# Thirty-four matmuls of a zeroed tile in TensorE's queue around the first scores

## The chip, the cores and the metric

The kernel runs on one core of one Trainium2 chip, in one launch. The metric is the device time of an execution in microseconds (us); the kernel before was timed three times.

## The reference

The layer takes x (8 batches, 8 heads, 512 tokens of 64) and a state of 32 rows for each batch and head, and computes in three steps:

```
scores  = x @ state.T / 8        a  = softmax(scores)     xread = a  @ state
scores2 = state @ x.T / 8        a2 = softmax(scores2)    sread = a2 @ x
x1 = concat(xread, sread) over tokens: (8, 544, 512), heads side by side
h  = relu(pad(x1) @ w_in);  conv = 3-tap convolution of h over tokens
x2 = (h * sigmoid(conv)) @ w_out
xk, xr = mixes of x2 with itself one token earlier (mu_k, mu_r)
out = sigmoid(xr @ w_r) * (relu(xk @ w_k)**2 @ w_v)
```

There are 512 + 32 = 544 tokens in a batch. Everything is float32.

## The kernel before, in words

Every large product is made of three matmuls (`mm3`, lines 108 to 114): each operand is split into a high and a low part, and high x high (L112), high x low (L113) and low x high (L114) are added up in PSUM. So each weight block has to be split before it is used (`Weights.split`, L158 to L170: two passes on ScalarE, the others on VectorE), and each intermediate too.

Phase 1 goes over nine tiles of tokens t (one for each batch, and one for all sread rows) and eight blocks f of the hidden size: a slot (t, f). The attention of a batch is folded into the first product: `m` (tile p_m) is state x w_in, and hps = m.T @ a gives the hidden block without ever forming xread. A slot is `g1_main` (hps), `g1_a` (ReLU, L430, and the taps, L441 and L443), `g1_b` (the gate), `g1_c` (the split) and `g1_sec` (the product with w_out into the four acc tiles). Phase 2 does the same for the last step, with kps, ks, acc and rps.

The attention of a batch (class `Attention`): `scores` (L284) multiplies the state's columns with x_t, four heads into each of two tiles p_s, g = 0 and 1. x_t of a batch comes in four transfers (L200), two heads in each. The code takes heads 0, 4, 1, 5 and so on, which is chunk 0, 2, 0, 2, 1, 3, 1, 3. Each score is two matmul instructions, 16 in all. VectorE then transposes p_s in blocks (L305), takes maxima (L296, L308), subtracts, sums, and turns the result back (L340, L343) into `aring`, which hps reads.

PSUM has eight banks: four acc tiles, two of hps or kps, and a ring of two under the tag "at" (`Attention.at`), for p_m, transposes and sread, and for scores of later batches; the first scores borrow two acc tiles. `m_odd` is the SBUF tile of the blocks m of odd batches, first written for batch 1.

What sets the order: the code is a list of instructions with priorities. The Tile framework plans it with a simulation that has its own costs and sends, on each engine, the instruction that is due first among those that are ready. In the prologue (L614 to L644) the due times count up in the order of the code; in the main loop they are written: slot number x 1000 plus the stage's offset `STAGE` (0 for the main product, 5400 for `g1_sec` and `g2_sec`), or 500 x half-slot less a lead for attention and weights, all behind BASE. So the prologue is due before all else; where one of its instructions is not ready, a later one that is goes first. On the chip each engine then works off its queue in the order planned.

The prologue, in order: loads of state and x_t of batch 0, the first w_in block, conv, mu and the first w_out block (L614 to L619, all issued by SyncE); the identity (`make_identity`) and zeros for `aux` on GpSimd; then

```
    a = Attention(0, ap)
    a.scores([ps_acc.tile([P, 512], F32, tag=f"acc{g}", name="p_s") for g in range(G)])
    a.begin()
    win[0][1]()
    a.state()
    a.m(0, 0, 1)
```

that is the scores, a small memset, the split of w_in, the split of the state (into `aux`), and the first block of m; then the softmax of both tiles, the split of conv and the split of w_out.

Of the kernel before, what the change touches and what calls it, by code (L numbers as in the profile page):

```python
# [8 lines left out]
F32 = mybir.dt.float32  # L9
# [15 lines left out]

ATTEND = 3
M_PARTS = (-8, -4, 3, 8)


@with_exitstack  # L30
def tile_kernel(
# [26 lines left out]
    nc = tc.nc  # L58
    B, P, NST, H, D = x_n.shape
# [10 lines left out]
    N = 512  # L70
# [31 lines left out]
    m_odd = xp.tile([P, KF // 2, 2, G, 2 * P], F32R, tag="x16", name="m_odd")  # L102
# [497 lines left out]
    def at_half(k, *fns, prio=None):  # L600
        p = 500 * k - AHEAD if prio is None else prio
        half.setdefault(k, []).extend((fn, p) for fn in fns)
# [14 lines left out]
    vec.load()  # L617
    nc.sync.dma_start(out=muc, in_=mu)
    wout[0][0]()  # L619
    make_identity(nc, ident)  # L620
    nc.gpsimd.memset(aux[:, 1].bitcast(F32), 0.0)
    a = Attention(0, ap)
    a.scores([ps_acc.tile([P, 512], F32, tag=f"acc{g}", name="p_s") for g in range(G)])
    a.begin()
    win[0][1]()
    a.state()
    a.m(0, 0, 1)
# [18 lines left out]
    def attend(b, k, first):  # L646

        a_ = a if first else Attention(b, ap)
        if not first:
            at_half(k, a_.begin, a_.scores)  # L650
            if b == 1:
                at_half(M_PARTS[0] + 2 * KF - 1, a_.state)
            at_half(k + 1, lambda: a_.max1(0, nc.vector), lambda: a_.max1(1, nc.gpsimd))
# [6 lines left out]
            h = 2 * KF * b  # L660
            for q, d in enumerate(M_PARTS):
                if b == 1:
# [142 lines left out]
```

## Time and profile before

| | |
|---|---|
| three timed runs | 898.67, 899.1, 899.33 us, median 899.1 |
| profiled execution | 901.15 us, of which 899.2 are the span |
| TensorE, busy | 850.8 us of 4440 matmuls (95%) |
| VectorE / ScalarE / GpSimd, busy | 564.0 / 531.2 / 118.8 us |
| granted TensorE clock, mean | 0.974 of 2.4 GHz |

The profile is one execution. PE is TensorE's matmul side and PEld its weight loads, DVE is VectorE, ACT ScalarE, POOL GpSimd, SP SyncE. The span runs from the first to the last instruction; all times in rows are us from its start. A bracket at the end of a row gives how long the engine was idle before it, and what ended that. The chain of waits is followed back from the last instruction, at each step to what released it. Matmuls are pipelined: the distance between the starts of two is what one costs in a dense stream, and it is shorter than the duration of one.

### The profile page before, as it was taken

The numbers are of one execution on the slowest core, as the hardware profiler recorded it, in microseconds if no ns is written. First come the engines' busy times: TensorE is split into PE (matmuls) and PEld (weight loads), VectorE is DVE, ScalarE is ACT, GpSimd is POOL, SyncE is SP. The second block draws the span as 40 slices with busy tenths as digits, with TensorE's granted clock in tenths as the row PEclk, the third lists the DMA queues.
The fourth block names the chain that finished last, engine by engine and source line by source line (L and its number), as shares of the span: only waits on it lengthen the run. The fifth ranks groups of instructions, "written<-read, shape, count | busy, mean of one in ns | idle before, by whom it ended". The sixth has DMA issues, their size and how long they took to land.

```text
span 899.2 us, 12003 instructions
## 1 busy us (share of the span) xinstructions
PE 850.8 (95%) x4440; PEld 692.3 (77%) x4440; DVE 564.0 (63%) x950; ACT 531.2 (59%) x929; POOL 118.8 (13%) x223
## 2 busy tenths in 40 slices
PE   3749999999999997999999999999999999999997
PEld 1628777768777875789988888888888888888886
DVE  6899897699879987999784543523424244332221
ACT  4557686578577757777666755635556364553431
POOL 2313753342011112121000000000000000000000
PEclk7778999999999999999999999999999999999999
DMA  9682224544451537536731101111001111011010
GB/s 341 228 348 96 77 95 118 162 131 118 139 166 59 168 127 246 175 122 252 273 128 47 28 20 47 47 47 48 18 29 48 47 47 47 1 36 48 0 47 36
DMA packets 50842, 95.76 MB, mean 106 GB/s; under 512 B 9056, under 2 KB 31072, under 8 KB 48736
## 3 DMA queue, kind: packets, MB, share of 16 engines
q1 hardware_dynamic: 50784, 95.00, 32.0%
q8 instruction: 35, 0.57, 0.3%
q14 instruction: 23, 0.19, 0.1%
HBM read 64.54 MB, written 17.86 MB: 92 GB/s over the span
## 4 chain that ended last, share of the span: by engine, by line
PE 83%; DVE 8%; ACT 3%; issue 2%; DMA 2%; POOL 1%; SPq 0%; DVEq 0%; ACTq 0%; POOLq 0%
PE acc L113 13%; PE acc L114 13%; PE acc L112 13%; PE kps L112 7%; PE kps L113 7%; PE kps L114 7%; PE rps L114 3%; PE rps L113 3%; PE rps L112 3%; PE hps L112 3%; PE hps L114 3%; PE hps L113 3%; DVE cacc L443 2%; PE p_s L284 2%; PE p_m L113 1%
## 5 line engine op out<-in xcount | busy, mean ns | idle before, releaser
L568 DVE TENSOR_TENSOR ks<-k,ks 128x512 fp32r<-128x512 f32 (+1 forms) x72 | 47.7, 662 | 118.2 <-ACT ks L567 117.8
L443 DVE SCALAR_TENSOR_TENSOR cacc<-hb,vcol,cacc 128x512 f32<-128x512 f32 (+1 forms) x144 | 111.8, 788 | 15.5 <-ACT cacc L441 14.9
L113 PE MATMUL acc<-gs,out 128*128 128x512 f32 (+1 forms) x288 | 110.6, 386 | 0.0
L112 PE MATMUL kps<-xk,k 128*128 128x512 f32 (+1 forms) x288 | 110.0, 384 | 0.2 <-ACT k L554 0.2
L113 PE MATMUL kps<-xk,k 128*128 128x512 f32 (+1 forms) x288 | 110.2, 382 | 0.0
L114 PE MATMUL kps<-xk,k 128*128 128x512 f32 (+1 forms) x288 | 109.8, 382 | 0.0
L114 PE MATMUL acc<-gs,out 128*128 128x512 f32 (+1 forms) x288 | 109.6, 384 | 0.0
L112 PE MATMUL acc<-v,ks 128*128 128x512 f32 x272 | 106.0, 392 | 0.0
L113 PE MATMUL acc<-v,ks 128*128 128x512 f32 x272 | 105.9, 389 | 0.0
L114 PE MATMUL acc<-v,ks 128*128 128x512 f32 x272 | 105.7, 392 | 0.0
L112 PE MATMUL acc<-gs,out 128*128 128x512 f32 (+1 forms) x288 | 94.3, 389 | 4.3 <-ACT gs L459 4.3
L533 DVE SCALAR_TENSOR_TENSOR mix<-yt,muc,mix 128x384 f32<-128x384 f32 (+7 forms) x128 | 61.1, 500 | 47.7 <-ACT mix L531 47.2
L567 ACT ACTIVATE ks<-k 128x512 fp32r<-128x512 f32 (+1 forms) x72 | 43.6, 605 | 69.8 <-PE acc L114 69.6
L531 ACT ACTIVATE mix<-yt,om 128x384 f32<-128x384 f32 (+7 forms) x128 | 61.5, 517 | 32.2 <-DMA yt<-y 15.8
L554 ACT ACTIVATE k<-kps 128x512 f32<-128x512 f32 (+1 forms) x72 | 40.9, 569 | 48.9 <-PE kps L114 48.7
L112 PEld LDWEIGHTS acc<-gs,out 128*128 128x128 f32 x288 | 53.7, 192 | 16.1 <-ACT gs L459 6.1
L113 PEld LDWEIGHTS acc<-gs,out 128*128 128x128 f32 x288 | 54.8, 190 | 12.8 <-POOL hb L429 0.8
L114 PEld LDWEIGHTS acc<-gs,out 128*128 128x128 f32 x288 | 54.9, 191 | 10.8 <-issue 0.8
L112 PEld LDWEIGHTS kps<-xk,k 128*128 128x128 f32 x288 | 54.1, 188 | 10.8 <-ACT k L554 0.7
L113 PEld LDWEIGHTS kps<-xk,k 128*128 128x128 f32 x288 | 54.4, 189 | 10.1
L114 PEld LDWEIGHTS kps<-xk,k 128*128 128x128 f32 x288 | 54.3, 188 | 10.1
L451 ACT ACTIVATE g<-cacc 128x512 f32<-128x512 f32 (+1 forms) x72 | 43.8, 609 | 27.5 <-DVE cacc L443 19.4
(133 smaller groups left out, 1771.3 us busy)
## 6 DMA issues: line engine op xcount, KB each, us to landing
out<-r SPq DMA_DIRECT2D x34, 256.0 KB, 2.1
xT<-x_t SPq DMA_DIRECT2D x32, 256.0 KB, 4.0
xn<-x_n SPq DMA_DIRECT2D x8, 1024.0 KB, 5.4
y<-yo SPq DMA_DIRECT2D x8, 1024.0 KB, 4.8
me<-m SPq DMA_DIRECT2D x48, 128.0 KB, 2.4
m_odd<-m SPq DMA_DIRECT2D x48, 128.0 KB, 2.4
raw<-w_in SPq DMA_DIRECT2D x8, 512.0 KB, 6.0
raw<-w_out SPq DMA_DIRECT2D x8, 512.0 KB, 5.7
```

What stands on the lines that cost most here:

```text
L112: nc.tensor.matmul(ps, lh, rh, start=start and k == 0, stop=False)
L113: nc.tensor.matmul(ps, lh, rl, start=False, stop=False)
L114: nc.tensor.matmul(ps, ll, rh, start=False, stop=stop and k == last)
L284: nc.tensor.matmul(self.v["s", g][NS * j:NS * (j + 1), :], sT[self.b][r, h // 2, h % 2], xT[self.b][r, h // 2], start=True, stop=True,)
L443: nc.vector.scalar_tensor_tensor(a[:, :n], hb[:, k:k + n], w[k], a[:, :n], op0=ALU.mult, op1=ALU.add)
L451: nc.scalar.activation(g[:, :n], s["a"][:, :n], AF.Sigmoid)
L531: nc.scalar.activation(tmp[:, o:o + m], y[:, c, q - 1:q - 1 + m], AF.Copy, scale=om[:, i:i + 1])
L533: nc.vector.scalar_tensor_tensor(tmp[:, o:o + m], y[:, c, q:q + m], muc[:, i:i + 1], tmp[:, o:o + m], op0=ALU.mult, op1=ALU.add,)
L554: nc.scalar.activation(k[:, :n], s["p"][:, :n], AF.Relu)
L567: nc.scalar.activation(ks[:, 0, :n], s["k2"][:, :n], AF.Copy)
L568: nc.vector.tensor_tensor(ks[:, 1, :n], s["k2"][:, :n], ks[:, 0, :n].bitcast(F32), op=ALU.subtract)
```

## The change

A slice of `m_odd`, which nothing has written yet, is zeroed on GpSimd ahead of the identity. A function `idle(n)` takes a tile of the ring "at" and issues n matmuls of the zeroed slice with itself into it, 128x128 weights and 512 columns each, none of which is read. It is called with 4 ahead of the first scores and with 30 behind `a.begin()`. Nothing else is changed.

```diff
+IDLE_BEFORE, IDLE_AFTER = 4, 30
...
     wout[0][0]()
+    zeros = m_odd[:, 3].rearrange("p l g n -> p (l g n)")
+    nc.gpsimd.memset(zeros[:, :N].bitcast(F32), 0.0)
+
+    def idle(n):
+        p = a.at("p_z")
+        for i in range(n):
+            nc.tensor.matmul(p, zeros[:, :P], zeros[:, :N], start=True, stop=True)
+
     make_identity(nc, ident)
     nc.gpsimd.memset(aux[:, 1].bitcast(F32), 0.0)
     a = Attention(0, ap)
+    idle(IDLE_BEFORE)
     a.scores([ps_acc.tile([P, 512], F32, tag=f"acc{g}", name="p_s") for g in range(G)])
     a.begin()
+    idle(IDLE_AFTER)
     win[0][1]()
     a.state()
```

## Rows read from the trace of the kernel before

**Rows 1.** The page's first part: busy time, share of the span, instructions.

```profile
PE 850.8 (95%) x4440; PEld 692.3 (77%) x4440; DVE 564.0 (63%) x950; ACT 531.2 (59%) x929; POOL 118.8 (13%) x223
```

**Rows 2.** Chain of waits, 0 to 50 us: start, duration, what.

```profile
1.18 2.81 DMA xT<-x_t
...
4.12 5.53 PE p_s L284 x16
...
20.29 1.15 DVE in L170
...
21.48 0.48 PE p_m L113
...
26.44 0.53 PE hps L112
...
30.06 0.61 ACT hb L430
```

**Rows 3.** Timeline of VectorE: start, duration, instruction, idle time before it.

```profile
6.73 0.72 DVE L305 STREAM_TRANSPOSE q<-p_s 128x512 f32<-128x512 f32 x1 [6.73 <-PE p_s L284]
...
9.68 0.72 DVE L305 STREAM_TRANSPOSE q<-p_s 128x512 f32<-128x512 f32 x1 [1.07 <-PE p_s L284]
...
31.53 0.75 DVE L443 SCALAR_TENSOR_TENSOR cacc<-hb,vcol,cacc 128x512 f32<-128x512 f32 x1 [2.04 <-ACT cacc L441]
```

**Rows 4.** Stretches: us, busy time of five engines, granted clock, DMA.

```profile
12.00:13.00 1.00, 0.00 (x0) 0.00 (x0) 0.97 (x4) 1.00 (x2) 0.00 (x0) 1.00 1.05 398
...
14.00:15.00 1.00, 0.00 (x0) 0.00 (x0) 1.00 (x4) 1.00 (x5) 0.00 (x0) 0.50 0.99 397
```

**Rows 5.** Tile p_s, first scores and those near 50 us: ns min/median/max, starts.

```profile
L284 PE MATMUL p_s<-xT,sT x16: 1027/1057/1059, 4.1 to 8.6; 64*32 64x512 f32 x16
...
L284 PE MATMUL p_s<-xT,sT x16: 589/589/613, 49.3 to 50.6; 64*32 64x512 f32 x16
```

**Rows 6.** Timeline of TensorE's weight loads, 4 to 8.5 us.

```profile
4.76 0.18 PEld L284 LDWEIGHTS p_s<-xT,sT 64*32 64x32 f32 x4 [0.45 <-DMA xT<-x_t]
6.44 0.19 PEld L284 LDWEIGHTS p_s<-xT,sT 64*32 64x32 f32 x4 [1.50 <-DMA xT<-x_t]
7.71 0.18 PEld L284 LDWEIGHTS p_s<-xT,sT 64*32 64x32 f32 x4 [1.08 <-DMA xT<-x_t]
```

**Rows 7.** Timeline of TensorE's matmuls, 28 to 32 us.

```profile
28.48 0.63 PE L112 MATMUL hps<-aring,me 128*128 128x512 f32 x1
...
29.76 0.63 PE L112 MATMUL hps<-aring,me 128*128 128x512 f32 x1
...
31.18 0.39 PE L112 MATMUL hps<-aring,me 128*128 128x512 f32 x1
...
31.64 0.40 PE L114 MATMUL hps<-aring,me 128*128 128x512 f32 x1
```

**Rows 8.** Timeline of GpSimd, 0 to 3.2 us.

```profile
0.73 0.20 POOL masks.py:197 MEMSET ident<- 128x128 f32 x1 [0.29 <-POOLq L794]
0.87 1.81 POOL L621 MEMSET aux<- 128x2048 f32 x1
2.62 0.13 POOL L293 MEMSET s<- 128x1 f32 x2
2.78 0.29 POOL masks.py:199 TENSOR_SCALAR_AFFINE_SELECT ident<-ident 128x128 f32<-128x128 f32 x1
```

**Rows 9.** TensorE, 400 to 557.1 us: matmuls of tile kps, then of ks.

```profile
400.00:557.10 157.10, 63.55 (x276) 1.00 0.35 123
...
400.00:557.10 157.10, 46.82 (x192) 1.00 0.35 123
```

**Rows 10.** Timeline of TensorE's matmuls, 17 to 18 us.

```profile
17.63 0.69 PE L112 MATMUL p_m<-in,aux 128*128 128x128 f32 x2 [8.00 <-DVE in L165]
```

**Rows 11.** Timeline of VectorE, then of TensorE, 66 to 75.2 us.

```profile
66.77 0.42 DVE L275 TENSOR_TENSOR me<-p_m,me 128x256 fp32r<-128x256 f32 x1
...
74.92 0.39 PE L114 MATMUL hps<-aring,me 128*128 128x512 f32 x1
```

## The prediction, made before the change was run

> **What bounds the kernel now.** Read the busy table of the page first: TensorE has 95% of the span [rows 1], so nearly all the time is a dense matmul stream, and 34 more matmuls can shorten nothing in that stream itself. The change sits in front of that stream, so next comes the chain of waits over the first 50 us: a transfer of x_t until 3.99, the 16 score matmuls until 9.65, then VectorE (DVE) work, the first scaled weights at 20.29 to 21.44, the first m block on TensorE from 21.48, the first hps product from 26.44, and the first ReLU at 30.06 [rows 2]. In VectorE's timeline its idle time is in brackets: the second scores keep it waiting 1.07 us before 9.68; from there it is never idle until 29.49, and then waits 2.04 us for the ScalarE result behind the first hps product [rows 3]. So up to 29.49 the prologue is paced by VectorE, which starts when the scores end; a microsecond taken from the scores moves all of it.
>
> Why the scores end at 9.65 is seen in two views. The rows of the scores' weight loads give the landings of the four chunks of x_t: 4.12 for the first [rows 2], and loads that ended an idle time at 4.76, 6.44 and 7.71 [rows 6]. So 1.94 us pass between the last landing and the end. And one score matmul of that stretch lasts 1057 ns where the same tile at 49 to 51 us lasts 589 [rows 5]. The first ones therefore ran at the lower of the two levels, 1.2 GHz, although the page prints a granted clock of 1.00 for the start. The stretch at 12 to 13 us reads 1.00 with TensorE idle, that at 14 to 15 reads 0.50 [rows 4]: the clock reached 2.4 GHz when the scores were over and was lost before the m blocks; from 28.48 to 29.76 three hps matmuls still take 0.427 us each from start to start, from 31.18 to 31.64 two take 0.23 each [rows 7].
>
> **The change part by part.** It removes nothing. It adds one memset on GpSimd (POOL) and 34 matmuls of 128x512 on TensorE; two tiles of the two-buffer PSUM ring "at" receive them.
>
> *The memset.* 128x512, ahead of the identity. The nearest rows are a 128x128 memset of 0.20 us and a 128x2048 one of 1.81 [rows 8]: these are the ends, and I take a quarter of the larger, 0.45. GpSimd starts at 0.73, so the tile is zero at about 1.2 and the first zero matmul can start at 1.3 (2.6 at the upper end). The identity, aux and the rest move back by 0.45; nobody on TensorE needs them before 17 us. Cost on the path: nothing.
>
> *What a zero matmul costs.* Its shape is that of hps: 0.427 us from start to start at the lower level, 0.23 at the upper [rows 7]. Its weight load has the shape of theirs and is hidden as theirs is. All 34 take 7.8 us at the upper level and 14.5 at the lower.
>
> *Where they stand.* The planner orders each engine's queue: of the instructions that are ready, the one that is due first. Both halves show in the rows. The scores stand in the queue chunk by chunk, as they land, not in the order of the code (which takes chunks 0 and 2 by turns), so ready work passes work that waits. And due times hold: before 557.1 us there are 276 kps matmuls (23 slots of 12) and 192 that read ks (8 slots of 9 and 10 of 12, so 18 slots), and kps of slot 23 (due 23000) comes just ahead of acc of slot 18 (due 18000 + 5400) [rows 9]. So all zero matmuls, those written behind the scores as well, may fill TensorE's wait before the scores: from 1.3 to 4.12 there is room for 2.8 / 0.427 = 6.6, so I put seven there. The seventh ends at 1.3 + 7 x 0.427 = 4.29, 0.17 late for the first chunk; that is covered, since the third lands only at 6.44. The other 27 run between or behind the scores.
>
> *The scores.* What it is worth depends on when the clock rises. No score matmul was quick, so it rose no sooner than 9.65, 5.5 us behind the first of them [rows 2, 5]; from the first hps matmul at 26.44 [rows 2] to the shorter spacing at 31.18 [rows 7] it took less than 4.8. From 1.3 that is 6.1 to 6.8 us, before the last chunk's landing at 7.71. Two passes of that chunk at the upper level: the second starts half of (1.94 - 1.06) later, 0.44, and lasts 0.59, so the scores end at 7.71 + 0.44 + 0.59 = 8.74 instead of 9.65: 0.9 us less. The ends: 0 (the clock rises after 9.65) and 0.9, since no landing moves.
>
> *Behind the scores.* 27 x 0.23 = 6.2 us: TensorE is busy until 8.74 + 6.2 = 15.0. Before the change it had nothing to do until 17.63 [rows 10], so no zero matmul holds anything up there. The second "at" buffer is free at 15.0, before the second m block wants it. Then 5.6 us pass until the m blocks go on at 21.48 - 0.9 = 20.6. Before the change the clock read 0.50 by 14 to 15 us, 4 to 5 us behind the last score [rows 2, 4], so it will be down again, and the m blocks and the first hps run at the lower level as now. I take nothing for them (bounds: 0 and the 2.04 of VectorE's wait).
>
> *What becomes late.* VectorE's g1 chain starts at 8.78; its g0 work, from 6.73 to 8.61, still fits in front. The weights' transfers do not move with the scores, so they are what could be late next; VectorE shows no wait between 9.68 and 29.49 [rows 3], so each was there in time, by how much these rows don't say: 0 to 0.9 of the gain passes, and I take 0.9. Behind 21.48 the chain goes from engine to engine [rows 2] and hands it on to the dense stream.
>
> *Sum.* The profiled execution took 901.15 us (span 899.2, 1.95 around it): 901.15 - 0.9 = 900.25. The three timed runs have a median of 899.1, 2.05 lower; on that scale 898.2.
>
> **Rivals.**
> *A. Most of the 34 stand ahead of the scores (slower).* Place: TensorE's queue before 9.65. For it: the planner does send instructions ahead of a busy engine. On GpSimd the aux memset (1.81 us) went out before the select that finishes the identity, and so did two small s memsets that come later in the code; the select can't have been ready, though the engine was busy long enough [rows 8]. Against it: the due-time order on TensorE [rows 9], which a deep queue filled on readiness would not keep. Price with all 34 in front: 5.5 us at the lower level hold 12.9, the other 21.1 take 4.9, so the scores start at 1.3 + 5.5 + 4.9 = 11.7 and end some 1.9 later (the 16 at 49.3 to 51.2 [rows 5]), at 13.6: VectorE's g1 work is 3.9 late. Its 2.04 of idle time takes part of that up, its g0 work (1.9, until now done before 8.61) is late as well: 1.9 to 3.8 are left; about +2.8, 901.9. It decides from where more zero matmuls are ahead than fit before 9.65 - 1.9 = 7.75 (12.9 in 5.5 us, and 0.95 / 0.23 = 4.1 more): some 17.
> In the Trainium skill, TensorE: Matmul & The Clock Gate, Part 3, "The mechanism", says that matmuls start and end strictly in program order and only weight loads are pulled ahead. The trace agrees: an hps matmul (L114) whose low half was written by 67.19 starts at 74.92, behind the m blocks that stand ahead of it [rows 11]. By that rule no score can overtake a zero matmul.
> *B. The clock stays up through the m blocks and the first hps (faster).* Then VectorE's 2.04 us at 29.49 go as well: 0.9 + 2.04 = 2.9, 896.2. For it: zero matmuls may stand later than I put them. Against: the 5.6 us without work.
> *C. The planner reorders what follows.* It plans with its own times of the prologue; if these change, so can the orders behind it. One such wait removed or added is worth what such waits cost now, VectorE's 1.07 and 2.04 [rows 3]: 897.0 or 900.6 from 898.2 with one, and about 896 or 901.5 with several; either sign, nothing in the profile speaks for one.
> *D. Nothing happens:* the clock rises too late for the last chunk, 899.1.
>
> **How the numbers follow.** A measurement can tell about 0.2%, 1.8 us, from no change: faster is below 897.3, slower above 900.9. Forecast 0.40 (faster 0.06, same 0.30, slower 0.04; its own range 896.9 to 899.6); A 0.17 (slower 0.145, same 0.025); B 0.15 (faster 0.135, same 0.015); C 0.25 (faster 0.14, slower 0.11); D 0.03 (same 0.02, slower 0.01). Together faster 0.335, same 0.36, slower 0.305. The range leaves out the far parts of A, B and C: 895.6 to 902.
>
> **What would show it.** Right: about seven zero matmuls at 0.43 us from 1.3 us on, score matmuls of the last chunk of about 0.59 us instead of 1.06, VectorE's second transpose near 8.8, the m block near 20.6 with 0.50 granted, VectorE's L170 for w_out ending at 28.6. Wrong: more than 17 zero matmuls before the first score and a second transpose later than 9.68 (A); hps at a spacing of 0.23 at its start (B); queues of the same engine in another order behind 30 us (C).

## The result

The kernel after takes 904.99 us (median of six runs, 903.22 to 907.47) against 899.22 of before (six runs): a ratio of 1.0059, 95% interval 1.0040 to 1.0079. It is 5.3 us slower by the ratio; 898.2 was forecast, with a range of 895.6 to 902.

The page of after, first part, answers to [rows 1]; the profiled execution took 905.28 us, its span 903.3:

```profile
PE 863.6 (96%) x4474; PEld 699.7 (77%) x4474; DVE 564.6 (63%) x950; ACT 532.6 (59%) x931; POOL 123.1 (14%) x224
```

Line numbers of after are two above those of before in the functions named here. Its timeline of TensorE, 0 to 38 us (start, duration, instruction, count; in brackets the idle time before it):

```profile
1.31 8.15 PE L628 MATMUL p_z<-m_odd 128*128 128x512 f32 x22 [1.31 <-POOL m_odd L623]
9.39 1.94 PE L286 MATMUL p_s<-xT,sT 64*32 64x512 f32 x16
11.26 3.02 PE L628 MATMUL p_z<-m_odd 128*128 128x512 f32 x12
19.13 0.66 PE L114 MATMUL p_m<-in,aux 128*128 128x128 f32 x2 [4.85 <-DVE in L167]
25.74 0.47 PE L115 MATMUL p_m<-in,aux 128*128 128x128 f32 x1 [5.95 <-DVE in L172]
...
35.15 1.22 PE L114 MATMUL hps<-aring,me 128*128 128x512 f32 x2 [1.60 <-ACT aring L344]
...
37.10 0.63 PE L114 MATMUL hps<-aring,me 128*128 128x512 f32 x1
37.53 0.63 PE L115 MATMUL hps<-aring,me 128*128 128x512 f32 x1
```

22 of the 34 zero matmuls stand ahead of the first score and 12 behind the last. The scores begin at 9.39 instead of 4.12 and end at 11.33 instead of 9.65 [rows 2], although they are quick now, as tile p_s shows (ns min/median/max):

```profile
L286 PE MATMUL p_s<-xT,sT x16: 589/589/613, 9.4 to 10.7; 64*32 64x512 f32 x16
```

VectorE's timeline of after answers to [rows 3]:

```profile
12.74 0.69 DVE L162 TENSOR_SCALAR raw<-raw 128x1024 f32<-128x1024 f32 x1 [12.74 <-ACT raw L160]
13.35 0.77 DVE L171 TENSOR_SCALAR mid<-mid 128x1024 uint32<-128x1024 uint32 x2
...
14.10 0.71 DVE L307 STREAM_TRANSPOSE q<-p_s 128x512 f32<-128x512 f32 x1
...
15.31 0.70 DVE L307 STREAM_TRANSPOSE q<-p_s 128x512 f32<-128x512 f32 x1
...
28.76 1.16 DVE L172 SCALAR_TENSOR_TENSOR out<-mid,raw 128x1024 fp32r<-128x1024 uint32 x1
...
34.13 0.69 DVE L162 TENSOR_SCALAR raw<-raw 128x1024 f32<-128x1024 f32 x1 [1.14 <-ACT raw L160]
```

The first of these is no softmax work. VectorE's queue has a different order: the split of w_in (its passes L162 and the larger L171) stands first, and the first transpose, for which the scores were ready by 11.33 at the latest, waits behind it until 14.10. What the split waits for is in the chain of waits of after (start, duration, what); it is a transfer, and the same wait stands there without the zero matmuls (order of after, below):

```profile
4.02 7.48 DMA raw<-w_in
11.58 1.13 ACT raw L160
...
13.35 0.28 DVE mid L171
...
14.19 0.62 DVE q L307
...
24.55 1.13 DVE in L172
```

So there are two differences to tell apart: the matmuls in TensorE's queue (scores 1.7 us late), and new orders on all queues (second transpose 5.6 late). By the order of the two traces, at least 120 of TensorE's 4440 matmuls (the zero matmuls left aside) and 81 of VectorE's 950 instructions stand elsewhere, and at least 42 of ScalarE's and 20 of GpSimd's; instructions alike in shape and tile can't be told apart, so these are lower bounds. Followed through the two traces, after is 9.2 us late at the first ReLU, 4.5 early at the fifth, 3.7 late at 140 us, and 2.8 to 2.9 late at the landmarks from 187 to 356 us; from 440 us to the end it is about 4.1. The last 1.3 is no finding: two profiles of the same order (before, and the control below) differ by 1.4 over that stretch, and against the control's profile after is 4.4 late at 187 us and 4.3 at the end. So the loss is made in the first 190 us, where TensorE is starved; the dense stream hands it on. How far TensorE has come by the end of the starved part is one row of a view by stretches (us; busy time and count of PE, PEld, DVE, ACT, POOL; granted clock; DMA share, GB/s). Before, then after:

```profile
0.00:145.00 145.00, 109.75 (x665) 83.84 (x666) 128.05 (x195) 90.73 (x146) 57.04 (x83) 0.86 0.55 195
```

```profile
0.00:145.00 145.00, 116.68 (x653) 87.58 (x654) 124.12 (x192) 89.55 (x144) 59.06 (x82) 0.87 0.54 191
```

Without the zero matmuls that is 665 of the kernel's own matmuls by 145 us before and 619 after; VectorE had worked 3.9 us less.

### The profile page after: what moved, and what is told of

It is laid out like the page before. It is cut to its first block, busy times and chain, and to the rows that moved or that the text cites. A ratio compares the mean times of both kernels' runs of the same rounds, so it can differ in the third digit from the quotient of the medians.

```text
span 903.3 us, 12066 instructions
## 1 busy us (share of the span) xinstructions
PE 863.6 (96%) x4474; PEld 699.7 (77%) x4474; DVE 564.6 (63%) x950; ACT 532.6 (59%) x931; POOL 123.1 (14%) x224
## 4 chain that ended last, share of the span: by engine, by line
PE 82%; DVE 8%; ACT 4%; DMA 3%; issue 1%; SPq 1%; DVEq 0%; ACTq 0%
PE acc L114 13%; PE acc L116 13%; PE acc L115 13%; PE kps L114 7%; PE kps L115 7%; PE kps L116 7%; PE rps L116 3%; PE rps L115 3%; PE rps L114 3%; PE hps L114 3%; PE hps L116 3%; PE hps L115 3%; DMA raw<-w_in 2%; PE p_s L286 1%; DVE cacc L445 1%
## 5 line engine op out<-in xcount | busy, mean ns | idle before, releaser
L445 DVE SCALAR_TENSOR_TENSOR cacc<-hb,vcol,cacc 128x512 f32<-128x512 f32 (+1 forms) x144 | 109.2, 771 | 9.8 <-ACT cacc L443 9.2
```

The source lines that it names most:

```text
L445: nc.vector.scalar_tensor_tensor(a[:, :n], hb[:, k:k + n], w[k], a[:, :n], op0=ALU.mult, op1=ALU.add)
```

## The experiments

**How the queues were held.** To change the matmuls without the order, or the order without the matmuls, the program is planned once to read off each engine's order, and then built a second time with each queue chained in an order of choice; the zero matmuls are put into TensorE's chain at a given place.

```diff
+    queues = program(PLAN, None)[1]          # the order that the planner lays
+    nc, order = program(IDLE, queues)        # built again in that order
...
+                        line = z[:first] + line[:8] + z[first:] + line[8:]
+                    for one, two in zip(line, line[1:]):
+                        tc.add_manual_dep(two, one.name, ...)
```

Lines of these kernels are six above those of before: L290 are the scores, L311 the transpose, L164 to L176 the weights' split. Ratios are to runs of the kernel before on the same chip.

**Order and matmuls, one at a time.** Four kernels: the order of before with nothing in it (the control), the order of before with 22 and 12 zero matmuls, the order of after with none, and the order of before with the forecast's 7 and 27.

```diff
-PLAN, IDLE, AHEAD_OF_SCORES = (0, 0), (0, 0), 0      # pin_before
+PLAN, IDLE, AHEAD_OF_SCORES = (0, 0), (4, 30), 22    # pin_b22
+PLAN, IDLE, AHEAD_OF_SCORES = (4, 30), (0, 0), 0     # pin_a0
+PLAN, IDLE, AHEAD_OF_SCORES = (0, 0), (7, 27), 7     # pin_b7
```

> The queues of the kernel before laid down by hand and nothing else: a control for the way in which the other runs fix their queues. Both theories: the time of the kernel before, 899.2, within 0.2%. If it is off by more, fixing the queues costs something itself, and the other runs are read against this one.

> Every engine keeps the queue of the kernel before, instruction by instruction; the zero matmuls stand as in the kernel after, 22 ahead of the scores and 12 behind. The theory of the position (the zero matmuls alone hold the scores and everything behind them): scores end at 11.3 instead of 9.65, and the whole loss comes with them, 904 to 906. The theory of the order (the planner laid the other queues differently, and that is the larger part): only the 1.7 us of the scores come, 900.9, or less where VectorE's second transpose was not the only thing late, 899.5 to 901.

> Every engine keeps the queue of the kernel after, but no zero matmul is in it (nor the memset of their tile). The theory of the order: the loss stays nearly whole, 903 to 905, VectorE still begins with the split of w_in near 12.7. The theory of the position: the loss goes with the matmuls, 899 to 900.5.

> The queues of the kernel before, with 7 zero matmuls ahead of the scores and 27 behind: the case that was forecast. By the forecast scores end at 8.7, VectorE's second transpose begins near 8.8, the m blocks stay at the lower clock, and the time is 898.2. If the 0.9 us is absorbed by VectorE's later waits, 899.2. If the clock stays up through the m blocks, 896 to 897.

| kernel | median, us | ratio to before | 95% |
|---|---|---|---|
| order of before, no zeros | 899.91 | 1.0000 | 0.9988 to 1.0012 |
| order of before, 22 + 12 | 901.61 | 1.0018 | 1.0008 to 1.0028 |
| order of after, no zeros | 906.67 | 1.0067 | 1.0048 to 1.0087 |
| order of before, 7 + 27 | 899.28 | 0.9990 | 0.9980 to 1.0001 |

The control costs nothing. The order of after costs 0.67%, 6.0 us, without one zero matmul; with them it is the kernel after, 0.59%, and the two intervals overlap. The 22 + 12 matmuls alone cost 0.18%, 1.6 us (0.7 to 2.5). By the point values the two make 7.6, more than the 5.3 of both together, but not beyond their intervals. TensorE, then VectorE, in the order of before with 22 + 12:

```profile
1.31 7.24 PE L635 MATMUL p_z<-m_odd 128*128 128x512 f32 x22 [1.31 <-POOL m_odd L628]
8.47 1.92 PE L290 MATMUL p_s<-xT,sT 64*32 64x512 f32 x16
```

```profile
9.60 0.72 DVE L311 STREAM_TRANSPOSE q<-p_s 128x512 f32<-128x512 f32 x1 [9.60 <-PE p_s L290]
...
11.41 0.70 DVE L311 STREAM_TRANSPOSE q<-p_s 128x512 f32<-128x512 f32 x1
```

The scores end at 10.39, 0.7 later than in before; the second transpose, which here follows the work on the first tile without a wait, is 1.73 us later than the 9.68 of before (2.4 later than in the control), and the timed runs lose 1.6. The traces don't show it handed on whole: against the control this one is 2.4 late at the first ReLU and 0.4 at 187 us. In the order of after without the zero matmuls, the scores run as before, and VectorE is late all the same:

```profile
4.11 5.50 PE L290 MATMUL p_s<-xT,sT 64*32 64x512 f32 x16 [4.11 <-DMA xT<-x_t]
```

```profile
12.10 0.70 DVE L166 TENSOR_SCALAR raw<-raw 128x1024 f32<-128x1024 f32 x1 [12.10 <-ACT raw L164]
...
14.67 0.71 DVE L311 STREAM_TRANSPOSE q<-p_s 128x512 f32<-128x512 f32 x1
```

The scores end at 9.61 there and wait 3.9 us for a VectorE that waits for ScalarE. The order is the larger part.

**Where in the order.** Three kernels without zero matmuls take one plan up to a cut and the other behind it, and one takes into the order of before a single thing from after: the start of VectorE's and ScalarE's queues.

```diff
+    one, two = (program(plan, None)[1] for plan in PLANS)
+    queues = {e: one[e][:CUT[e]] + two[e][CUT[e]:] for e in one}
...
+    for e, (skip, n) in {"EngineType.DVE": (0, 4), "EngineType.Activation": (2, 1)}.items():   # pin_bd4
+        early = after[e][skip:skip + n]
+        rest = [k for k in queues[e] if k not in early]
+        queues[e] = rest[:skip] + early + rest[skip:]
```

> No zero matmul. The queues of the kernel before, with one thing from the kernel after: w_in's first split (one instruction of ScalarE, four of VectorE) stands ahead of the first softmax maxima, so VectorE begins with it and waits for the weight's landing. The start: VectorE's second transpose slips from 9.7 to about 15 and all behind it, 904 to 906. The middle: the slip of 5 to 6 us is partly taken up by VectorE's later waits, 901 to 903, or wholly, 899.6.

> No zero matmul. Every engine keeps the queue of the kernel after up to some 53 us (VectorE's first 69 instructions, TensorE's first 166, ScalarE's 45, GpSimd's 23, SP's 38), and the queue of the kernel before from there on. The theory of the start (VectorE's late begin, 12.7 instead of 6.7, is the price of the planner's order): the loss is nearly whole, 904 to 907. The theory of the middle (the price is paid by the order further on, where the second ReLU groups and the w splits stand): 899 to 901.5, since at 45 us the order of after stood 3.8 us ahead at the second p_s.

> No zero matmul. As the run before, but the queues of the kernel after hold up to some 97 us (VectorE 131, TensorE 370, ScalarE 82, GpSimd 39, SP 45 instructions), those of the kernel before from there on. The start: 904 to 907, as in the run before. The middle: here the loss comes, 902 to 907, and the difference to the run before is the part paid between 53 and 97 us. If both give 899.5 to 901, the loss sits behind 97 us.

> No zero matmul. The reverse: the queues of the kernel before up to some 53 us, those of the kernel after from there on. The start: the loss is gone, 899 to 901. The middle: the loss stays, 903 to 907.

| kernel | median, us | ratio to before | 95% |
|---|---|---|---|
| before, w_in's split first | 905.50 | 1.0061 | 1.0041 to 1.0081 |
| after to 53 us, then before | 909.39 | 1.0099 | 1.0078 to 1.0120 |
| after to 97 us, then before | 903.44 | 1.0042 | 1.0028 to 1.0056 |
| before to 53 us, then after | 911.93 | 1.0127 | 1.0100 to 1.0153 |

The start alone is enough for the whole loss. Five instructions moved to the front (three of w_in's split, L164 on ScalarE, L166 and the larger L175 on VectorE; the other two, of 0.17 us each, belong to conv and mu), and VectorE begins at 13.45 with the split:

```profile
13.45 0.69 DVE L166 TENSOR_SCALAR raw<-raw 128x1024 f32<-128x1024 f32 x1 [13.45 <-ACT raw L164]
...
16.61 0.70 DVE L311 STREAM_TRANSPOSE q<-p_s 128x512 f32<-128x512 f32 x1
```

That is 6.9 us late at the second transpose, and 5.5 us (0.61% of 900.24) at the end. The cuts gave more than was expected of them, and answer less: by the medians a cut at 53 us costs more than either whole plan in both directions (1.0099 and 1.0127 against 1.0067; the first interval still overlaps with that of after's order). So a cut can cost something itself, and the loss cannot be read off as a sum of stretches. Only the cut at 97 us lies between the plans, with 0.42% against 0.67% and intervals that overlap; how much of the loss is paid by then is not shown.

The reverse of the start, in the order of after, puts six softmax instructions into VectorE's idle time:

```diff
+    soft = [dve[n] for n in (4, 6, 7, 8, 10, 12)]
+    queues["EngineType.DVE"] = soft + [n for n in dve if n not in soft]
```

> No zero matmul. The queues of the kernel after, but VectorE's first six softmax instructions (two transposes, four maxima) stand ahead of w_in's first split, in the time in which VectorE idles. The theory of the start: 3.9 us of work go into the idle time, 906.7 falls to 902 to 903.5. The rival, that the price of the planner's order lies further on alone: 906 to 907.

It took 903.99 (1.0048, 1.0029 to 1.0068). VectorE began with the transposes, at 8.35, and had done 3.9 us of softmax work when it came to w_in's split:

```profile
8.35 1.37 DVE L311 STREAM_TRANSPOSE q<-p_s 128x512 f32<-128x512 f32 x2 [8.35 <-PE p_s L290]
...
12.21 0.70 DVE L166 TENSOR_SCALAR raw<-raw 128x1024 f32<-128x1024 f32 x1
```

By the medians the loss to before on the same chip falls from 7.0 to 4.5 us, by the ratios from 6.0 to 4.3; 1.7 to 2.5 come back, less than the 3.2 to 4.7 expected, and the two intervals overlap, so that any comes back is not sure. 4.3 us or more are left in an order whose start is now good. So a late start is enough for such a loss in the order of before, but in the order of after the order further on costs as well.

**The planner, with other counts.** In these kernels the planner lays all queues itself. The matmuls written behind the scores may only be issued once the last score is, so that the count ahead is the one named; with a count of 0 the call is left out.

```diff
-IDLE_BEFORE, IDLE_AFTER = 4, 30     # in after's trace 22 ahead, 12 behind
+IDLE_BEFORE, IDLE_AFTER = 4, 30     # four30
+IDLE_BEFORE, IDLE_AFTER = 7, 27     # seven27
+IDLE_BEFORE, IDLE_AFTER = 4, 0      # ahead4
+IDLE_BEFORE, IDLE_AFTER = 0, 30     # behind30
...
-    idle(IDLE_AFTER)
+    with tc.issue_after(a.last.ins):
+        idle(IDLE_AFTER)
```

> The planner lays all queues anew, but the 30 matmuls traced behind the scores may only be issued once the last score is: 4 zero matmuls ahead, 30 behind, as the change's text has them. The theory that the 22 ahead are the trigger (they push the scores in the planner's own account past w_in's landing, and so it puts the split first): VectorE begins with the transposes as before, 898 to 901. The rival that any zero matmul makes the planner lay a worse order: 903 to 907.

> As the run before, with 7 ahead and 27 behind: the count that was forecast, with the planner's own order of the rest. The trigger theory: 898 to 901, within 1 us of the same counts in the queues of before (899.3). The rival: 903 to 907. A spread of over 2 us between this run and the one with 4 and 30 would say that the planner's order of the rest is worth that much by itself.

> 4 zero matmuls ahead of the scores, none behind; the planner lays the queues anew. They end before x_t's first chunk has landed, so on the chip they can cost nothing themselves. If a new plan is a draw: anywhere from 899 to 907, and VectorE's begin does not tell which. If only a late begin of VectorE costs: 899 to 900.

> No zero matmul ahead, 30 behind the scores, where TensorE idles until 17.6 us; the planner lays the queues anew. If a new plan is a draw: anywhere from 899 to 907. If only a late begin of VectorE or matmuls ahead of the scores cost: 898.5 to 900.

| zero matmuls ahead, behind | median, us | ratio to before | 95% |
|---|---|---|---|
| 4, 30 | 905.17 | 1.0064 | 1.0046 to 1.0082 |
| 7, 27 | 901.16 | 1.0013 | 0.9996 to 1.0029 |
| 4, 0 | 901.91 | 1.0021 | 1.0010 to 1.0032 |
| 0, 30 | 903.00 | 1.0030 | 1.0012 to 1.0048 |

Here the account of the late start fell. All four begin VectorE's work with the transposes, and with 4 and 30 the second is as early as in the control (8.97):

```profile
7.21 0.72 DVE L307 STREAM_TRANSPOSE q<-p_s 128x512 f32<-128x512 f32 x1 [7.21 <-PE p_s L286]
...
9.01 0.70 DVE L307 STREAM_TRANSPOSE q<-p_s 128x512 f32<-128x512 f32 x1
```

and it is still as slow as after; against the control it is level at 47 us, 1.6 late at 52 and 4.2 to 5.9 late from 75 to 88. The lateness is first seen at the scores of batch 1. In the control all 16 follow one another; with 4 and 30 four hps matmuls stand between two groups of eight, and the first group begins 2.6 us later. TensorE with 4 and 30, then in the control:

```profile
51.22 1.06 PE L286 MATMUL p_s<-xT,sT 64*32 64x512 f32 x8 [0.67 <-DVE me L277]
...
53.34 1.06 PE L286 MATMUL p_s<-xT,sT 64*32 64x512 f32 x8
```

```profile
48.66 1.92 PE L290 MATMUL p_s<-xT,sT 64*32 64x512 f32 x16 [1.02 <-DVE sr L377]
```

Whether the order or the matmuls cost it was settled by holding that order and leaving the matmuls out:

> Every engine keeps the queue that the planner laid for 4 zero matmuls ahead and 30 behind, but none of them is in it, nor the memset. The theory of the order: 904 to 906.5, as with them. The theory of the matmuls (they, or their tile's memset and bank, hold something): 899 to 900.5.

It took 907.23 (1.0074, 1.0054 to 1.0093), no less than with them. So it is the order again. With 4 ahead and none behind, the last zero matmul ends at 3.39, before the first chunk of x_t lands, and the kernel still costs 0.21%. That its plan costs this is argued: the plan without the four was not run. By their ratios none of the five kernels with a plan laid around zero matmuls is as good as that of before; they lie between 0.13% and 0.64% above it, and the interval of the best, 7 and 27, includes 1.

How far TensorE had come goes roughly with the loss. The kernel's own matmuls by 145 us, from the view by stretches: 665 before and 672 in the control; 677 in before's order with 7 + 27 (-0.10%), 665 with 22 + 12 (+0.18%), 660 with 4 and 0 (+0.21%), 636 in after's order with six softmax instructions first (+0.48%), 628 with the cut at 97 us (+0.42%), 621 with 4 and 30 (+0.64%) and 608 in that order alone (+0.74%), 619 after (+0.59%), 613 in its order alone (+0.67%) and with the split first (+0.61%), 605 and 601 with the cuts at 53 us (+0.99%, +1.27%). It is not exact: 625 with 7 and 27 cost only 0.13%, 618 with 0 and 30 only 0.30%.

**A longer bridge.** In the order of before, with 7 ahead, 54 behind keep TensorE working until the m blocks.

```diff
-IDLE = (7, 27)
+IDLE = (7, 54)
```

> The queues of the kernel before, 7 zero matmuls ahead of the scores and 54 behind instead of 27, so that TensorE works until about 20 us, when w_in's first split is ready: a case beyond the forecast (clock up through the m blocks). If the m blocks then run at the higher clock and VectorE's wait of 2 us near 31 shrinks: 896 to 898.5. If the clock falls all the same, or the gain is taken up later: 899.3, as with 27. If the first m matmuls, now behind the zeros, come late: 900 to 901.

It took 898.45 against 899.46 of before on its chip: 0.9982, 0.9971 to 0.9993, the one kernel here whose interval lies below 1; one of 15 kernels, and so small a gain, is weak evidence. With 27 behind, TensorE's m blocks are 0.21 us apart, with 54 they are 0.11, and VectorE's wait of 2.04 before the first taps [rows 3] is gone (0.41 is the first idle time left near it). TensorE with 27:

```profile
1.30 3.36 PE L635 MATMUL p_z<-m_odd 128*128 128x512 f32 x7 [1.30 <-POOL m_odd L628]
4.59 3.12 PE L290 MATMUL p_s<-xT,sT 64*32 64x512 f32 x16
7.64 6.46 PE L635 MATMUL p_z<-m_odd 128*128 128x512 f32 x27
...
20.41 0.41 PE L120 MATMUL p_m<-in,aux 128*128 128x128 f32 x1
20.62 0.41 PE L118 MATMUL p_m<-in,aux 128*128 128x128 f32 x1
```

and with 54, TensorE and then VectorE:

```profile
20.97 0.27 PE L119 MATMUL p_m<-in,aux 128*128 128x128 f32 x1
21.08 0.27 PE L120 MATMUL p_m<-in,aux 128*128 128x128 f32 x1
```

```profile
28.75 1.53 DVE L449 SCALAR_TENSOR_TENSOR cacc<-hb,vcol,cacc 128x512 f32<-128x512 f32 x2
30.69 0.70 DVE L166 TENSOR_SCALAR raw<-raw 128x1024 f32<-128x1024 f32 x1 [0.41 <-ACT raw L164]
```

The first taps (L449) come 1.4 us earlier than with 27, but at the ReLUs near 76 and 81 us the trace with 54 is 1.0 and 1.5 us behind the other, and from 132 us on the two are level to 0.2: what VectorE gained there is lost again. Whether 54 is better than 27 these runs don't tell, as the intervals overlap.

## Why the prediction was wrong

*What bounds the start: right in the main.* A late VectorE costs most of what it is late: 6.9 us late cost 5.5 (w_in's split first). With 22 + 12 in the order of before, 1.7 late cost 1.6, but with an interval of 0.7 to 2.5. VectorE's wait of 1.07 for the second scores [rows 3] belongs to that one profile: in the control, with 22 + 12 and with 7 + 27 the second transpose follows the first by 1.8 us without a wait, so there the end of the first tile's scores sets the start, and not the last landing.

*The memset and the price of a zero matmul: right.* The memset took 0.52 us (0.45 was taken), the first zero matmul began at 1.31 (1.3). Seven took 3.29 from 1.30 to the first score at 4.59, 0.47 each; the 27 behind the scores took 0.24 each.

Two steps failed.

*Where they stand: wrong, the smaller of the two.* The prediction let the planner fill TensorE's wait before the scores as it is on the chip, with seven. It put 22 there; why 22 is not shown, as the planner's own account of that wait is in no profile. The bound of 17 from which rival A decides was passed, and the form of A came true: in after the scores end 1.7 us late. In the order of before, 22 + 12 end them 0.7 late, VectorE's second transpose is 1.7 late, and the price is 1.6 us. The Trainium skill, TensorE: Matmul & The Clock Gate, Part 3, "The mechanism", has matmuls start strictly in program order; the traces agree: with 22 put ahead in the order of before no score begins until 8.47, behind the last of them, though in before the first chunk was there at 4.12 [rows 2].

*The scores: right in form, and in part by luck.* With 7 and 27 in the order of before they run at 589 to 613 ns from 4.59 on and end at 7.71, and VectorE's second transpose begins at 8.24. From the first load of the last chunk (6.66) to the end 1.05 us pass, where 1.03 were forecast; that the end is 1.0 earlier than the forecast 8.74 is the landing, which came 1.05 earlier than in before. But the upper level came before 4.59 there, not at 6.1 to 6.8. In the two other profiles with 7 ahead it came later, as tile p_s shows (7 + 27 and 7 + 54 in the order of before, then the plan with 7 and 27):

```profile
L290 PE MATMUL p_s<-xT,sT x16: 589/601/613, 4.6 to 7.1; 64*32 64x512 f32 x16
...
L290 PE MATMUL p_s<-xT,sT x16: 590/1057/1059, 4.6 to 7.7; 64*32 64x512 f32 x16
...
L286 PE MATMUL p_s<-xT,sT x16: 589/968/1059, 4.6 to 7.5; 64*32 64x512 f32 x16
```

There VectorE's second transpose begins at 9.04 and 8.99, no earlier than the control's 8.97. The time with 7 and 27 is 0.9990 of before, 0.9 us less, which was the forecast's gain, with an interval from 1.8 less to 0.1 more: a gain is not shown. The second transpose of before, at 9.68, is 0.7 later than the control's in the same order, so the first microseconds vary by that much from run to run.

*Behind the scores: right.* With 7 and 27 TensorE is idle from 14.1 to 16.4, and the m blocks run at the lower level, as forecast. The rival that the clock stays up (B) did not come with 34; with 61 it did, and the whole kernel gained 0.18%, 1.6 us, not 2.9. What the clock gave of that is not shown, as 7 and 27 without it gained 0.10%.

*The planner reorders what follows (C): the larger step that failed.* The sum has no term for new orders on the other queues; it keeps VectorE's rows of before, so they stand in it at nothing. Only rival C has them, right in its mechanism and mis-sized in its price: one or a few waits of 1.07 and 2.04, to about 901.5, either sign. (Its 897.0 and 900.6 for one wait don't follow from 898.2 and these waits, which give 896.2 to 897.1 and 899.3 to 900.2.) Measured, the order of after alone costs 6.0 us. Two things were missing from that price. A reordered queue can put ready work behind an instruction that waits for a transfer: VectorE began at 12.74, not 6.73, which is 6 us later, while the two waits of the price are the longest that before's VectorE has between 6.73 and 32 us. And the sign was not even: all five kernels with plans laid anew were slower by their point value.

That the planner puts w_in's split first because 22 zero matmuls push the scores back in its own account is argued, not shown: with 0, 4 and 7 ahead it did not, and no count between 7 and 22 was run. Why the plan with 4 and 30 is so much worse than that with 7 and 27 stays open.

## What to carry to other kernels

An instruction added to a planned kernel is two changes: what it does on its engine, and a new plan of all the others; price the second by what a reordered queue can block (here a whole transfer's wait), not by the waits that the present trace has, and expect a loss even where no such block shows (4 and 30). Hold the order of the kernel before and add the instruction to it, and hold the new order without the instruction: the two runs give the two prices. Filler that nothing ties can go ahead of the real work (here 22, where 4 were written ahead), so tie it to an instruction that it must follow.

## What was not expected of the hardware

The upper clock level came at different times in runs whose TensorE does the same work without a break from 1.30 or 1.31 us. With 7 ahead, the score matmuls from 4.59 on are all quick in one profile of three; in the two others their median is 1057 and 968 ns. With 22 ahead, a zero matmul takes 628 ns and more up to 4.89 us in the one kernel (order of before) and the next, from 5.31, only 482; in the other (after) it takes that up to 6.59, and the next, from 7.02, 585. So the level rose before 4.59 us in one run and after 7 in another, though both begin with the same seven matmuls.
